# Forgetting attention and a tanh-shrink MLP in one kernel: seven MLP steps in four slots, and transposed q and k landing in tiles of their own

## The chip, the core and the metric

One core of a Trainium2 chip runs the whole program. The engines are TensorE (PE: matmuls; PEld: its weight loads), VectorE (DVE), ScalarE (ACT), GpSimd (POOL) and SyncE (SP), which only issues DMAs here. The metric is the device time of one execution in microseconds.

## What is computed

The reference, cut down (B = 8 batches, H = 8 heads, S = 576 positions, D = 64, so 4608 tokens of width 512; w_in is 512 x 2048, w_out 2048 x 512):

```python
scores = np.matmul(q, k.transpose(0, 1, 3, 2)) / np.sqrt(D)
cum = np.cumsum(np.log(np.clip(f, 0.0001, 1.0)), axis=-1)
decay = cum[:, :, :, None] - cum[:, :, None, :]
attn = softmax(np.where(causal, -1e9, scores + decay))
x = (attn @ v).transpose(0, 2, 1, 3).reshape(B * S, H * D)
h = x @ w_in
out = (h - np.tanh(h)) @ w_out
```

## The kernel before

**Slots.** Attention runs over 32 pairs of heads, four pairs for each batch, in the order of `pairs`. The loop at the end (L368) has 33 slots, p = 0 to 32. In slot p stand the scores of pair p (seven tiles, `scores`), the values of pair p-1 (`values`) and the turning of that pair's result into XR (`turn`, L291), with features on the partitions. XR (L67) is a ring of four batches.

**Units and steps.** The MLP is cut into nine units of 512 tokens, and each unit into 32 steps: 16 `mlp1` steps (L306: four matmuls into hps, tanh on ScalarE as th, the sum on VectorE as gt) and then 16 `mlp2` steps (L322: four matmuls into ops; after each fourth step one copy by ScalarE and one DMA of out). The list `mlp` (L365) holds them in order. From slot 5 on, each slot takes the next eight (`take`, L373) and strews them between its attention items; what is left after slot 32 runs alone, the tail. With eight to a slot, unit u starts with the first step of slot 5 + 4u. It reads XR rows of batch u, whose last pair is turned in slot 4u + 4.

**Order.** The order on TensorE, VectorE, GpSimd and SyncE is the order of the program (`manual_schedule`), and each of them works its queue off in order. An instruction that waits holds up everything behind it on its engine.

**q and k.** A batch's q and k stand with head dimension on the partitions in QT and KT, two buffers each (b % 2): rows 0 to 63 the data, rows 64 to 66 the decay and constants that go with a 67-row matmul (`lhsT=KT[...][0:D + 3]`, L258). Batches 0 to 2 are transposed on TensorE and copied out by VectorE (`trans`, L218 to L236), in slots 0 to 10. Batches from FAR = 3 on come by DMA. With p0 = 4(b-1): GpSimd loads the blocks of q in slot p0-1 and of k in slot p0 (`load_block`); SyncE issues five transposing DMAs for q in slot p0 and five for k in slot p0+1 (`turn_block`, L87). These land two heads at a time, on 128 partitions of the even heads' places of QT and KT; in slot p0+2 VectorE moves the lower 64 rows to the odd heads' places (`odd_heads`, L91, eight copies of 64x576). Since the transposes overwrite rows 64 to 127 of the even heads, slot p0+3 puts the constant rows back (`even_rows`, L154, two DMAs) and loads the decay rows (`load_aug`, L148, three DMAs). The table LOADS (L186 to L214) says after which tile of which slot each of these is emitted.

Of the kernel before, what the change touches and what calls it, by code (L numbers as in the profile page):

```python
# [9 lines left out]
FP16 = mybir.dt.float16  # L10
# [4 lines left out]
PITCH = 640  # L15
# [6 lines left out]
def kernel(  # L22
# [10 lines left out]
    nc = tc.nc  # L33
    P = 128

    B, H, S, D = q.shape
# [4 lines left out]
    NPAIR = H // 2  # L41
# [10 lines left out]
    qkp = ctx.enter_context(tc.tile_pool(name="qkp", bufs=1))  # L52
# [18 lines left out]
    qn, kn = ([t[0:S // NT6, :].rearrange("p (h n d) -> p h n d", h=H, n=NT6) for t in raw] for raw in (qraw, kraw))  # L71
    qb, kb = ([t[:, 0:NJ * DM].rearrange("p (n e) -> p n e", n=NJ) for t in raw] for raw in (qraw, kraw))
    vn = [qkp.tile([P, NJ, H, VW], FP16, tag=f"vn{i}", name=f"vn{i}") for i in range(2)]
    QT = [qkp.tile([P, H, S], FP16, tag=f"QT{i}", name=f"QT{i}") for i in range(2)]
    KT = [qkp.tile([P, H, PITCH], FP16, tag=f"KT{i}", name=f"KT{i}") for i in range(2)]

    def load_qk(dst, src, b, h0, h1):
        nc.gpsimd.dma_start(
            out=dst[b % 2][:, h0:h1, :, :].rearrange("p h n d -> p h (n d)"),
            in_=src[b, h0:h1, :, :].rearrange("h (p n) d -> p h (n d)", n=NT6))  # L80

    def load_block(dst, src, b, n):
        pn = min(P, S - n * P)
        nc.gpsimd.dma_start(out=dst[b % 2][0:pn, n, :].rearrange("p (h d) -> p h d", h=H),  # L84
                            in_=src[b, :, n * P:n * P + pn, :].rearrange("h p d -> p h d"))

    def turn_block(dst, src, b, n):  # L87
        pn = min(P, S - n * P)
        nc.sync.dma_start_transpose(out=dst[b % 2][:, 0:H:2, n * P:n * P + pn], in_=src[b % 2][0:pn, n, :])

    def odd_heads(dst, b, c):  # L91
        nc.vector.tensor_copy(out=dst[b % 2][0:D, 2 * c + 1, 0:S], in_=dst[b % 2][D:P, 2 * c, 0:S])

    def load_v_rest(b):
        nc.gpsimd.dma_start(out=vn[b % 2][0:S % P, NJ - 1, :, 0:D],
                            in_=v[b, :, S - S % P:S, :].rearrange("h p d -> p h d"))

    def load_v_head(b, h):
        nc.gpsimd.dma_start(out=vn[b % 2][:, 0:NJ - 1, h, 0:D],
                            in_=v[b, h, 0:S - S % P, :].rearrange("(n p) d -> p n d", p=P))  # L100

    def load_v_block(b, n, h0, h1):
        nc.gpsimd.dma_start(out=vn[b % 2][:, n, h0:h1, 0:D],  # L103
                            in_=v[b, h0:h1, n * P:(n + 1) * P, :].rearrange("h p d -> p h d"))
# [11 lines left out]
    ones16 = cst.tile([NH, S], FP16)  # L116
    nc.vector.memset(ones16, 1.0)
    minus16 = cst.tile([2 * H, S], FP16)
# [11 lines left out]
    for i in range(2):  # L130
        nc.vector.memset(KT[i][:, :, S:PITCH], 0.0)
    cum = cst.tile([NH, S], FP32)
# [15 lines left out]
    def load_aug(b):  # L148
        i, hs = b % 2, slice(b * H, (b + 1) * H)
        nc.sync.dma_start(out=KT[i][D:D + 1, :, 0:S], in_=chi[hs, :])  # L150
        (nc.gpsimd if b == 0 else nc.sync).dma_start(out=QT[i][D + 2:D + 3, :, :], in_=cq[hs, :])
        nc.sync.dma_start(out=KT[i][D + 1:D + 2, :, 0:S], in_=clo[hs, :])

    def even_rows(i):  # L154
        nc.sync.dma_start(out=QT[i][D:D + 2, 0:H:2, :], in_=minus16[0:H, :])
        nc.sync.dma_start(out=KT[i][D + 2:D + 3, 0:H:2, 0:S], in_=ones16[0:H // 2, :])

    def const_rows(i):
        nc.sync.dma_start(out=QT[i][D:D + 2, :, :], in_=minus16)
        nc.sync.dma_start(out=KT[i][D + 2:D + 3, :, 0:S], in_=ones16[0:H, :])  # L160

# [16 lines left out]
    def load_win(f0, f1):  # L178
        nc.gpsimd.dma_start(out=win[:, :, f0:f1],
                            in_=moe_w_in[:, f0:f1].rearrange("(c p) f -> p c f", p=P))  # L180

    def load_wout(t0, t1):
        nc.gpsimd.dma_start(out=wout[:, t0:t1, :],
                            in_=moe_w_out[t0 * P:t1 * P, :].rearrange("(t p) e -> p t e", p=P))

    LOADS = {(0, 1): [lambda: load_qk(qn, q, 1, 0, 2), lambda: load_qk(kn, k, 1, 0, 2)],  # L186
             (0, 4): [lambda: load_qk(qn, q, 1, 2, H)],
             (1, 0): [lambda: load_qk(kn, k, 1, 2, H)],
             (1, 2): [lambda: load_win(0, DFF // 2)],
             (1, 5): [lambda: load_v_rest(1), lambda: load_v_head(1, 0)],  # L190
             (2, 1): [lambda: load_v_head(1, 1), lambda: load_win(DFF // 2, DFF)],
             (4, 0): [lambda: load_wout(0, NFT // 2)],
             (4, 2): [lambda: load_wout(NFT // 2, NFT)]}
# [4 lines left out]
    for b in range(2, B):  # L198
        p0 = (b - 1) * NPAIR
        for n in range(NJ - 1):  # L200
            LOADS.setdefault((p0 + 1, n), []).append(lambda b=b, n=n: load_v_block(b, n, 0, H))
        LOADS.setdefault((p0 + 1, 4), []).append(lambda b=b: load_v_rest(b))
        if b < FAR:
            LOADS.setdefault((p0, 0), []).append(lambda b=b: load_aug(b))
            continue
        for n in range(NJ):
            LOADS.setdefault((p0 - 1, n), []).append(lambda b=b, n=n: load_block(qb, q, b, n))
            LOADS.setdefault((p0, n), []).append(lambda b=b, n=n: load_block(kb, k, b, n))
            LOADS.setdefault((p0, 4), []).append(lambda b=b, n=n: turn_block(QT, qb, b, n))
            LOADS.setdefault((p0 + 1, 4), []).append(lambda b=b, n=n: turn_block(KT, kb, b, n))  # L210
        for c in range(NPAIR):
            LOADS.setdefault((p0 + 2, c), []).append(lambda b=b, c=c: odd_heads(QT, b, c))
            LOADS.setdefault((p0 + 2, 3 + c), []).append(lambda b=b, c=c: odd_heads(KT, b, c))
        LOADS.setdefault((p0 + 3, 0), []).append(lambda b=b: (even_rows(b % 2), load_aug(b)))  # L214

    E, XN, GT, M2 = {}, {}, {}, {}

# [30 lines left out]
    def scores(b, c, ti):  # L248
        ps = ps_sc.tile([P, 512], FP32, tag="sc", name="ps")
        if ti == LAST:  # L250
            e = EL[(b * NPAIR + c) % 3]
        else:
            e = aex.tile([P, 512], FP16, tag="e", name="e")
        lo = min(x[4] for x in TILES[ti])
        hi = max(x[4] + x[3] for x in TILES[ti])
        for a, j, i0, n, col in TILES[ti]:
            h = 2 * c + a
            nc.tensor.matmul(out=ps[:, col:col + n], lhsT=KT[b % 2][0:D + 3, h, j * P:(j + 1) * P],  # L258
                             rhs=QT[b % 2][0:D + 3, h, i0:i0 + n])
            for ib in range(j, NJ):  # L260
                w0 = min(ib * P, S - P)
                if i0 <= ib * P < i0 + n:
                    E[(b, c, a, j, ib)] = e[:, col + w0 - i0:col + w0 - i0 + P]
        nc.scalar.activation(out=e[:, lo:hi], in_=ps[:, lo:hi], func=AF.Exp, scale=qscale)  # L264
        col, cp, step, wd = MASKS[ti]
        view = e[:, col:col + (cp - 1) * step + wd]
        if cp == 1:
            pat = [[1, wd]]
        else:
            view = bass.AP(view.tensor, view.offset, [list(view.ap[0]), [step, cp], [1, wd]])  # L270
            pat = [[0, cp], [1, wd]]
        nc.gpsimd.affine_select(out=view, in_=view, compare_op=ALU.is_ge, fill=0.0,  # L272
                                base=0, pattern=pat, channel_multiplier=-1)
# [93 lines left out]
    with tc.manual_schedule(engines={PE, mybir.EngineType.Pool, mybir.EngineType.SP, mybir.EngineType.DVE}):  # L367
        for p in range(len(pairs) + 1):  # L368
            b, c = divmod(p, NPAIR)
            if p == 0:  # L370
                load_aug(1)
            items = att_items(p)
            take = 8 if p > NPAIR else 0  # L373
            mine = mlp[at:at + take]
            at += take
            first = 3 if p == NPAIR + 1 else 0
            given, n = 0, 0
            whole = sum(counts for _, counts in items)
            for emit, counts in items:
                emit()  # L380
                n += counts
                while n > first and given < len(mine) and given * (whole - first) < (n - first) * len(mine):
                    fn, *args = mine[given]
                    fn(*args)
                    given += 1
        for fn, *args in mlp[at:]:
            fn(*args)
# [28 lines left out]
```

## Time and profile before

| what | value |
|---|---|
| median of three runs | 377.35 us (376.13 to 380.36) |
| the profiled execution's own time | 376.38 us |
| its span, first to last instruction | 374.5 us |
| time outside the span | 1.88 us |
| mean granted TensorE clock | 0.981 |
| TensorE busy | 345.0 us, 92% of the span |
| VectorE, ScalarE, GpSimd busy | 190.8, 219.7, 162.5 us |

The span is what the trace covers; the execution's own time is 1.88 us more. A row of a list of groups gives source line, engine, operation and tiles (out<-in, with partitions x elements), its count, the total and the mean of one, and then the idle time of that engine just before it with the instruction that ended it. Matmul records overlap: a 128x512 matmul is listed with 378 ns, but in an unbroken row one starts each 216 ns (64 of them took 13.81 us), so an MLP step of four takes 0.86 us.

### The profile page before, as it was taken

What the parts mean: (1) busy time and instruction counts of PE and PEld (TensorE: products, weight loads), DVE (VectorE), ACT (ScalarE), POOL (GpSimd) and SP (SyncE); (2) the same over time, 40 slices, a digit from 0 to 9 for tenths busy, and PEclk for the clock granted to TensorE, in tenths of its full rate; (3) what the DMA queues carried; (4) which work ended last, traced back from release to release, by engine and by line L of the source; (5) the groups of instructions that cost most, each with busy time, mean ns of one, the idle gap of its engine ahead of it and who ended that gap; (6) DMA issues with size and microseconds to landing.
All of it is one profiled execution on the core that took longest, in us unless ns stands there. A gap on an engine that the chain in (4) does not pass through costs nothing.

```text
span 374.5 us, 7401 instructions
## 1 busy us (share of the span) xinstructions
PE 345.0 (92%) x2724; PEld 188.6 (50%) x2724; DVE 190.8 (51%) x352; ACT 219.7 (59%) x411; POOL 162.5 (43%) x340
## 2 busy tenths in 40 slices
PE   1778999989899999979998999799999999999995
PEld 0556555545445455545556865355555554444442
DVE  7589688448941584137613771069117612721720
ACT  6565576558745785568655865478558832623721
POOL 7978723655166636644475547552222210000000
PEclk9997699999999999999999999899999999999999
DMA  8999999999879996999599959994220022002002
GB/s 104 157 175 192 204 178 91 128 130 147 76 71 140 140 147 69 137 133 149 44 140 150 129 72 140 141 132 71 74 75 18 16 74 72 3 28 84 2 28 84
DMA packets 140801, 38.79 MB, mean 104 GB/s; under 512 B 128114, under 2 KB 135070, under 8 KB 140766
## 3 DMA queue, kind: packets, MB, share of 16 engines
q0 software_dynamic: 92416, 18.37, 65.5%
q1 hardware_dynamic: 48350, 19.96, 28.1%
q8 instruction: 21, 0.34, 0.4%
q14 instruction: 14, 0.11, 0.1%
HBM read 36.85 MB, written 9.44 MB: 124 GB/s over the span
## 4 chain that ended last, share of the span: by engine, by line
PE 73%; DVE 10%; DMA 9%; ACT 4%; issue 2%; POOL 2%; SPq 0%; POOLq 0%; ACTq 0%; DVEq 0%
PE ops L328 28%; PE hps L314 27%; PE ps L258 9%; PE av L282 8%; DMA XR<-xn 7%; DVE gt L320 3%; DVE KT L236 2%; ACT e L264 1%; ACT th L317 1%; DVE QT L236 1%; DVE xn L288 1%; ACT ost L332 1%; PE t L227 1%; DMA lf<-in_f_dram 1%; DMA KT<-clo 1%
## 5 line engine op out<-in xcount | busy, mean ns | idle before, releaser
L264 ACT ACTIVATE e<-ps 128x512 f16<-128x512 f32 x192 | 110.9, 596 | 70.0 <-PE ps L258 68.7
L314 PE MATMUL hps<-XR,win 128*128 128x512 f16 (+1 forms) x640 | 142.1, 360 | 7.6 <-DMA XR<-xn 7.2
L320 DVE TENSOR_TENSOR gt<-hps,th 128x512 f16<-128x512 f32 x144 | 98.1, 690 | 91.0 <-ACT th L317 89.8
L328 PE MATMUL ops<-wout,gt 128*128 128x512 f16 x576 | 138.4, 378 | 0.0
L272 POOL TENSOR_SCALAR_AFFINE_SELECT e<-e 128x128 f16<-128x128 f16 (+1 forms) x192 | 64.6, 339 | 128.8 <-ACT e L264 126.5
L317 ACT ACTIVATE th<-hps 128x512 f32<-128x512 f32 x144 | 86.4, 600 | 42.1 <-PE hps L314 34.0
L258 PE MATMUL ps<-QT,KT 67*128 67x64 f16 (+4 forms) x384 | 79.4, 289 | 10.9 <-DMA KT<-clo 4.4
L314 PEld LDWEIGHTS <-win 128*128 128x128 f16 x640 | 58.5, 98 | 51.4 <-issue 2.2
L328 PEld LDWEIGHTS <-gt 128*128 128x128 f16 x576 | 52.2, 97 | 54.1 <-issue 0.2
L258 PEld LDWEIGHTS <-KT 67*128 67x128 f16 x384 | 37.6, 101 | 56.0 <-issue 18.6
L332 ACT ACTIVATE ost<-ops 128x512 f32<-128x512 f32 x36 | 21.5, 597 | 36.3 <-PE ops L328 29.2
L282 PEld LDWEIGHTS <-e 128*128 128x128 f16 x896 | 34.9, 101 | 8.6 <-POOL e L272 2.4
L282 PE MATMUL av<-vn,e 128*128 128x65 f16 x896 | 36.3, 199 | 1.4 <-POOL e L272 1.4
L286 DVE TENSOR_SCALAR rs<-av 128x10 f32<-128x10 f32 x32 | 5.3, 165 | 58.6 <-PE av L282 58.5
L103 POOL DMA_DIRECT2D vn<-in_v_dram x32 | 28.0, 876 | 2.3 <-issue 1.7
L288 DVE TENSOR_TENSOR xn<-av,rs 128x640 f16<-128x640 f32 x32 | 26.4, 825 | 1.1
L84 POOL DMA_DIRECT2D kn<-in_k_dram x25 | 21.2, 847 | 2.0 <-issue 1.8
L84 POOL DMA_DIRECT2D qn<-in_q_dram x25 | 21.2, 848 | 1.9 <-issue 1.5
L236 DVE COPY QT<-t 64x576 f16<-64x576 f16 x22 | 17.7, 804 | 7.5 <-PE t L227 7.3
L236 DVE COPY KT<-t 64x576 f16<-64x576 f16 x24 | 19.1, 796 | 4.1 <-PE t L227 3.9
L282 PE MATMUL av<-vn,el 128*128 128x65 f16 x64 | 12.7, 199 | 0.0
L272 POOL TENSOR_SCALAR_AFFINE_SELECT el<-el 128x128 f16<-128x128 f16 x32 | 9.9, 308 | 5.2 <-ACT el L264 5.0
(44 smaller groups left out, 95.5 us busy)
## 6 DMA issues: line engine op xcount, KB each, us to landing
out_dram<-ost SPq DMA_DIRECT2D x36, 256.0 KB
vn<-in_v_dram POOLq DMA_DIRECT2D x24, 128.0 KB, 5.4
qn<-in_q_dram POOLq DMA_DIRECT2D x20, 128.0 KB, 4.5
kn<-in_k_dram POOLq DMA_DIRECT2D x20, 128.0 KB, 4.5
win<-in_moe_w_in_dram POOLq DMA_DIRECT2D x2, 1024.0 KB, 11.3
wout<-in_moe_w_out_dram POOLq DMA_DIRECT2D x2, 1024.0 KB, 13.2
XR<-xn SPq DMA_TRANSPOSE x56
vn<-in_v_dram POOLq DMA_DIRECT2D x12, 64.0 KB, 4.9
```

What stands on the lines that cost most here:

```text
L84: nc.gpsimd.dma_start(out=dst[b % 2][0:pn, n, :].rearrange("p (h d) -> p h d", h=H), in_=src[b, :, n * P:n * P + pn, :].rearrange("h p d - ...
L103: nc.gpsimd.dma_start(out=vn[b % 2][:, n, h0:h1, 0:D], in_=v[b, h0:h1, n * P:(n + 1) * P, :].rearrange("h p d -> p h d"))
L236: nc.vector.tensor_copy(out=to, in_=of)
L258: nc.tensor.matmul(out=ps[:, col:col + n], lhsT=KT[b % 2][0:D + 3, h, j * P:(j + 1) * P], rhs=QT[b % 2][0:D + 3, h, i0:i0 + n])
L264: nc.scalar.activation(out=e[:, lo:hi], in_=ps[:, lo:hi], func=AF.Exp, scale=qscale)
L272: nc.gpsimd.affine_select(out=view, in_=view, compare_op=ALU.is_ge, fill=0.0, base=0, pattern=pat, channel_multiplier=-1)
L282: nc.tensor.matmul(out=av[:, a, ib, :], lhsT=E.pop((b, c, a, j, ib)), rhs=vn[b % 2][:, j, 2 * c + a, 0:D + 1], start=(j == 0), stop=(j == ib))
L288: nc.vector.tensor_tensor(out=xn.rearrange("p i (a d) -> p a i d", a=2), in0=av[:, :, :, 0:D], in1=rs.to_broadcast([P, 2, NJ, D]), op=ALU. ...
L314: nc.tensor.matmul(out=hps[:, o:o + n], lhsT=win[:, ci, ft * P:(ft + 1) * P], rhs=XR[:, ci, t:t + n], start=(ci == 0), stop=(ci == NCH - 1))
L317: nc.scalar.activation(out=th, in_=hps, func=AF.Tanh, scale=-1.0)
L320: nc.vector.tensor_tensor(out=gt, in0=hps, in1=th, op=ALU.add)
L328: nc.tensor.matmul(out=ops, lhsT=GT[(u, ft)][:, m * P:(m + 1) * P], rhs=wout[:, ft, :], start=(ft == 0), stop=(ft == NFT - 1))
```

## The change

Three things. Slots 6 to 9 take seven MLP steps instead of eight, so that units 1 to 6 start in the middle of a slot, four steps later, and four more steps stand in the tail. The transposing DMAs land in two tiles of their own, TQ and TK (128 partitions, four pairs), each with one buffer; in slot p0+3 eight copies of VectorE (`place`) move them to rows 0 to 63 of QT and KT, even and odd heads, two heads at a time. So nothing overwrites rows 64 to 66 any more: `even_rows` is gone, and `load_aug` moves from slot p0+3 to slot p0. QT and KT have 67 partitions instead of 128.

```diff
@@ QT and KT are made @@
-    QT = [qkp.tile([P, H, S], FP16, tag=f"QT{i}", name=f"QT{i}") for i in range(2)]
-    KT = [qkp.tile([P, H, PITCH], FP16, tag=f"KT{i}", name=f"KT{i}") for i in range(2)]
+    QT = [qkp.tile([D + 3, H, S], FP16, tag=f"QT{i}", name=f"QT{i}") for i in range(2)]
+    KT = [qkp.tile([D + 3, H, PITCH], FP16, tag=f"KT{i}", name=f"KT{i}") for i in range(2)]
+    TQ = qkp.tile([P, NPAIR, S], FP16, tag="TQ", name="TQ")
+    TK = qkp.tile([P, NPAIR, S], FP16, tag="TK", name="TK")
@@ turn_block, odd_heads @@
-        nc.sync.dma_start_transpose(out=dst[b % 2][:, 0:H:2, n * P:n * P + pn], in_=src[b % 2][0:pn, n, :])
-
-    def odd_heads(dst, b, c):
-        nc.vector.tensor_copy(out=dst[b % 2][0:D, 2 * c + 1, 0:S], in_=dst[b % 2][D:P, 2 * c, 0:S])
+        nc.sync.dma_start_transpose(out=dst[:, :, n * P:n * P + pn], in_=src[b % 2][0:pn, n, :])
+
+    def place(dst, src, b, a, c):
+        nc.vector.tensor_copy(out=dst[b % 2][0:D, 2 * c + a:2 * c + 3 + a:2, 0:S], in_=src[a * D:(a + 1) * D, c:c + 2, :])
@@ even_rows is left out; LOADS @@
+        LOADS.setdefault((p0, 0), []).append(lambda b=b: load_aug(b))
         if b < FAR:
-            LOADS.setdefault((p0, 0), []).append(lambda b=b: load_aug(b))
             continue
...
-            LOADS.setdefault((p0, 4), []).append(lambda b=b, n=n: turn_block(QT, qb, b, n))
-            LOADS.setdefault((p0 + 1, 4), []).append(lambda b=b, n=n: turn_block(KT, kb, b, n))
-        for c in range(NPAIR):
-            LOADS.setdefault((p0 + 2, c), []).append(lambda b=b, c=c: odd_heads(QT, b, c))
-            LOADS.setdefault((p0 + 2, 3 + c), []).append(lambda b=b, c=c: odd_heads(KT, b, c))
-        LOADS.setdefault((p0 + 3, 0), []).append(lambda b=b: (even_rows(b % 2), load_aug(b)))
+            LOADS.setdefault((p0, 4), []).append(lambda b=b, n=n: turn_block(TQ, qb, b, n))
+            LOADS.setdefault((p0 + 1, 4), []).append(lambda b=b, n=n: turn_block(TK, kb, b, n))
+        for n, (dst, src) in enumerate(((QT, TQ), (KT, TK))):
+            for a in range(2):
+                for c in (0, 2):
+                    LOADS.setdefault((p0 + 3, 2 * n + a), []).append(lambda b=b, dst=dst, src=src, a=a, c=c: place(dst, src, b, a, c))
@@ the loop over slots @@
-            take = 8 if p > NPAIR else 0
+            take = 0 if p <= NPAIR else 7 if NPAIR + 1 < p <= 2 * NPAIR + 1 else 8
```

Two places show how this moves the instructions. First VectorE, for batch 4 (p0 = 12), before: slot 14 and the start of slot 15. The row with seven gt reaches back into slot 13; rs and xn are the values of one pair; QT_97 and KT_99 are the buffers of even batches.

```order
L320 TENSOR_TENSOR gt<-hps,th 128x512 x7
L92 COPY QT_97<-QT_97 64x576
...
L288 TENSOR_TENSOR xn<-av,rs 128x2x5x64
L320 TENSOR_TENSOR gt<-hps,th 128x512 x2
L92 COPY QT_97<-QT_97 64x576
L320 TENSOR_TENSOR gt<-hps,th 128x512
L92 COPY KT_99<-KT_99 64x576
L92 COPY QT_97<-QT_97 64x576
L320 TENSOR_TENSOR gt<-hps,th 128x512 x2
L92 COPY KT_99<-KT_99 64x576
L320 TENSOR_TENSOR gt<-hps,th 128x512
L92 COPY KT_99<-KT_99 64x576 x2
```

The same batch in the changed program, slot 15 (the seven gt begin in slot 14):

```order
L318 TENSOR_TENSOR gt<-hps,th 128x512 x7
L94 COPY QT_97<-TQ 64x2x576 x2
L318 TENSOR_TENSOR gt<-hps,th 128x512
L94 COPY QT_97<-TQ 64x2x576 x2
L284 TENSOR_SCALAR rs<-av 128x10
L285 RECIPROCAL rs<-rs 128x10
L286 TENSOR_TENSOR xn<-av,rs 128x2x5x64
L318 TENSOR_TENSOR gt<-hps,th 128x512 x2
L94 COPY KT_99<-TK 64x2x576 x4
```

Eight copies that stood scattered among the gt of slot 14 are now eight copies of twice the size, one slot later, in a slot with about four gt: two pairs around one gt, and four in a row behind the unit's last gt.

Second SyncE, in the slots 15 and 16 before (out_dram is a block of the result and ost its copy, XR<-xn the turning of a pair, QT_98<-qn_92 the first transposes for batch 5):

```order
L155 DMA QT_97<-minus_114 2x4x576
L156 DMA KT_99<-ones_112 1x4x576
L150 DMA KT_99<-chi 1x8x576
L151 DMA QT_97<-cq 1x8x576
L152 DMA KT_99<-clo 1x8x576
L334 DMA out_dram<-ost 128x512
L302 DMA_TRANSPOSE XR<-xn 128x4x128
L304 DMA_TRANSPOSE XR<-xn 128x64
L334 DMA out_dram<-ost 128x512 x2
L302 DMA_TRANSPOSE XR<-xn 128x4x128
L304 DMA_TRANSPOSE XR<-xn 128x64
L89 DMA_TRANSPOSE QT_98<-qn_92 128x4x128 x4
```

And in the changed program, from the turning in slot 15 through slot 16:

```order
L300 DMA_TRANSPOSE XR<-xn 128x4x128
L302 DMA_TRANSPOSE XR<-xn 128x64
L332 DMA out_dram<-ost 128x512
L152 DMA KT_100<-chi 1x8x576
L153 DMA QT_98<-cq 1x8x576
L154 DMA KT_100<-clo 1x8x576
L332 DMA out_dram<-ost 128x512
L300 DMA_TRANSPOSE XR<-xn 128x4x128
L302 DMA_TRANSPOSE XR<-xn 128x64
L91 DMA_TRANSPOSE TQ<-qn_92 128x4x128 x4
L91 DMA_TRANSPOSE TQ<-qn_92 128x4x64
L332 DMA out_dram<-ost 128x512 x2
```

The five small DMAs ahead of slot 15's turning are gone, and three of them (for the next batch) stand in slot 16. The turning of slot 16, which ends batch 3 and which unit 3 waits for, stands as before behind one block of the result that is copied in the middle of the slot; the unit's steps that read it come half a slot later.

More of the change, by code (lines that the diff above doesn't have):

```diff
@@ L152, in load_aug @@
         nc.sync.dma_start(out=KT[i][D + 1:D + 2, :, 0:S], in_=clo[hs, :])
-    def even_rows(i):
-        nc.sync.dma_start(out=QT[i][D:D + 2, 0:H:2, :], in_=minus16[0:H, :])
-        nc.sync.dma_start(out=KT[i][D + 2:D + 3, 0:H:2, 0:S], in_=ones16[0:H // 2, :])
     def const_rows(i):
@@ L257, in scores @@
             h = 2 * c + a
-            nc.tensor.matmul(out=ps[:, col:col + n], lhsT=KT[b % 2][0:D + 3, h, j * P:(j + 1) * P],
-                             rhs=QT[b % 2][0:D + 3, h, i0:i0 + n])
+            nc.tensor.matmul(out=ps[:, col:col + n], lhsT=KT[b % 2][:, h, j * P:(j + 1) * P],
+                             rhs=QT[b % 2][:, h, i0:i0 + n])
             for ib in range(j, NJ):
```

## The prediction

> **What bounds the kernel now.** I read the page's busy times first, then TensorE's waits, then where those waits lie, then the busy times by slot.
>
> ```profile
> PE 345.0 (92%) x2724; PEld 188.6 (50%) x2724; DVE 190.8 (51%) x352; ACT 219.7 (59%) x411; POOL 162.5 (43%) x340
> ```
>
> TensorE is the bound: it works 345.0 of 374.5 us. Only its 29.5 us of idle time, and time at a lowered clock, can be won. A step moved from one place to another, both limited by TensorE, wins nothing. The list of waits, for TensorE:
>
> ```profile
> PE hps L314 <- DMA XR<-xn: 7.2, 5, 2.2
> PE t L227 <- DMA qn<-in_q_dram: 5.0, 1, 5.0
> PE ps L258 <- DMA KT<-clo: 4.4, 1, 4.4
> PE ps L258 <- DVE KT L236: 4.0, 6, 1.6
> ```
>
> The 5.0 and the 4.4 are the first loads and stay. The 7.2 in five pieces and the 4.0 are what an order can change. The timeline of TensorE, cut to the instructions that waited, shows where they lie:
>
> ```profile
> 82.28 0.38 PE L314 MATMUL hps<-XR,win 128*128 128x512 f16 x1 [1.02 <-DMA XR<-xn]
> 91.66 0.39 PE L258 MATMUL ps<-QT,KT 67*128 67x512 f16 x1 [0.36 <-DVE KT L236]
> 99.66 1.02 PE L314 MATMUL hps<-XR,win 128*128 128x512 f16 x4 [0.28 <-DVE gt L320]
> 103.60 0.39 PE L258 MATMUL ps<-QT,KT 67*128 67x512 f16 x1 [1.62 <-DVE KT L236]
> 123.78 0.38 PE L314 MATMUL hps<-XR,win 128*128 128x512 f16 x1 [0.72 <-DMA XR<-xn]
> 163.04 0.38 PE L314 MATMUL hps<-XR,win 128*128 128x512 f16 x1 [2.19 <-DMA XR<-xn]
> 201.71 0.27 PE L314 MATMUL hps<-XR,win 128*128 128x256 f16 x1 [1.12 <-DMA XR<-xn]
> 240.90 0.47 PE L314 MATMUL hps<-XR,win 128*128 128x512 f16 x1 [2.10 <-DMA XR<-xn]
> ```
>
> The five waits for XR are the first steps of units 1 to 5, some 39 us (four slots) apart: three matmuls on the older pairs run, the fourth waits for the pair just turned. Around 90 to 104 us (slots 9 and 10) there are three others, all for VectorE, 2.26 us together. Busy times by stretch: slots 9, 10, 13, 14 and 16, each about from one pair's values to the next's:
>
> ```profile
> 84.20:95.00 10.80, 10.44 (x92) 5.56 (x90) 9.82 (x17) 8.59 (x17) 5.59 (x11) 1.00 1.70 146
> 95.00:105.94 10.94, 9.04 (x83) 4.80 (x82) 10.53 (x21) 7.14 (x14) 3.19 (x9) 1.00 0.49 47
> 125.25:134.48 9.23, 9.23 (x80) 4.89 (x77) 6.42 (x12) 7.63 (x16) 5.59 (x11) 1.00 1.68 146
> 134.48:143.73 9.25, 9.25 (x80) 4.88 (x77) 8.43 (x19) 7.45 (x15) 2.71 (x8) 1.00 0.58 85
> 152.96:164.50 11.54, 9.35 (x80) 4.87 (x77) 1.63 (x4) 5.18 (x10) 7.07 (x13) 1.00 1.34 135
> ```
>
> The columns are length, then busy time of PE, PEld, DVE, ACT, POOL, clock, DMA. An undisturbed slot is all TensorE, 9.23 of 9.23. Slots 9 and 10 are VectorE's (9.82 of 10.80 and 10.53 of 10.94): eight gt, the copies of a transposed pair and, in slot 10, the odd heads fall together. The slot ahead of a new unit is 11.54, its surplus the 2.19 of the wait.
>
> After the wait of 2.10 us the clock fell. Three neighbouring stretches there, and the one after the wait of 2.19:
>
> ```profile
> 237.40:240.81 3.41, 1.40 (x8) 0.60 (x7) 0.00 (x0) 1.71 (x4) 2.18 (x5) 1.00 1.87 151
> 240.81:244.20 3.39, 3.30 (x24) 1.81 (x24) 0.73 (x2) 1.68 (x3) 1.17 (x2) 0.53 1.28 149
> 244.20:247.60 3.40, 3.40 (x34) 1.94 (x32) 2.64 (x6) 1.80 (x4) 0.58 (x2) 0.96 1.01 147
> 162.80:166.20 3.40, 3.16 (x42) 2.00 (x42) 1.68 (x4) 1.68 (x3) 1.23 (x3) 1.00 1.75 134
> ```
>
> A granted clock of 0.53 over 3.39 us costs 0.47 x 3.39 = 1.6 us. One wait brought it, one just as long didn't.
>
> **The half slot: minus 7.2 and minus 1.6.** A unit's first mlp1 step comes four steps and one pair's values later: four steps of 0.86 us, 0.9 us of values and three scores of 0.2, about 5.0 us. XR keeps its place behind one block of the result that is copied in the middle of the slot. In slot 16, VectorE's and SyncE's rows:
>
> ```profile
> 154.37 0.82 DVE L288 TENSOR_TENSOR xn<-av,rs 128x640 f16<-128x640 f32 x1
> ```
> ```profile
> 156.94 1.22 SPq L302 DMA_TRANSPOSE XR<-xn  x1
> 158.21 1.40 SPq L304 DMA_TRANSPOSE XR<-xn  x1
> ```
>
> xn is ready at 155.2, the turning is issued from 156.94 to 159.6, and TensorE goes on at 163.04. The longest wait is 2.19, so the half slot leaves 5.0 - 2.2 = 2.8 us to spare. SyncE has new work ahead of it in that slot, the three decay rows:
>
> ```profile
> L150 SPq DMA_DIRECT2D KT<-chi x8: 634/634/662, 7.1 to 262.8; - x8
> ```
>
> 3 x 0.63 = 1.9 us from the slot's start, over before the block of the result that it waits for anyway (156.5), so it costs nothing here; with that cover gone, 1.9, still under 2.8. So all five waits go, 7.2 us, and with them the slow clock, 1.6. The four steps that slots 6 to 9 lose, 4 x 0.86 = 3.5 us, come back in the tail, which is all TensorE: zero. Only slot 6 is doubtful, where VectorE is nearly full; bounds 0 and +0.4, I take 0.
>
> The Trainium skill, in "TensorE: Matmul & The Clock Gate", Part 1, ties the slow clock to at least one idle window of about 3.4 us. The row above shows it after an idle piece of 2.10 us, so the trace is stricter than the page. If the page were right here, the dip would have another cause and could stay; that is the third rival.
>
> **Slots 9 and 10: minus 1.6.** Unit 1's mlp1 now takes half of slot 9, slot 10 and half of slot 11, and the odd heads of batch 3 leave slot 10 for slot 11, where no pair is transposed. Prices from the page's groups:
>
> ```profile
> L320 DVE TENSOR_TENSOR gt<-hps,th 128x512 f16<-128x512 f32 x144 | 98.1, 690 | 91.0 <-ACT th L317 89.8
> L236 DVE COPY KT<-t 64x576 f16<-64x576 f16 x24 | 19.1, 796 | 4.1 <-PE t L227 3.9
> L92 DVE COPY KT<-KT 64x576 f16<-64x576 f16 x20 | 6.5, 343 | 1.2 <-issue 0.5 <-DMA KT<-kn 0.3
> L288 DVE TENSOR_TENSOR xn<-av,rs 128x640 f16<-128x640 f32 x32 | 26.4, 825 | 1.1
> ```
>
> Slot 9 falls from eight gt to four, 2.8 us less; slot 10 loses 8 x 0.31 = 2.5 but keeps 8 x 0.69 + 4 x 0.80 + 1.2 for the values (0.825 and two short ones) = 9.9, still above TensorE's 9.04 there, and may hand some of it on to slot 11. Of the 2.26 us I count 1.6; bounds 0.5 and 2.3.
>
> **The copies: plus 1.0.** Forty copies of 64x576 become forty of 64x1152. No row has this shape. The nearest:
>
> ```profile
> L92 DVE COPY QT<-QT x20: 301/306/395, 94.3 to 258.7; 64x576 f16<-64x576 f16 x20
> L168 DVE COPY vn<-clo 64x1 f16<-64x1 f16 x4 | 0.3, 138 | 0.0
> ```
>
> Between 138 ns for one column and 301 for 576 lie 0.283 ns a column, which makes 138 + 1152 x 0.283 = 0.46 us. Slot 15 then has 8 x 0.46 = 3.7, about four gt (2.8) and the values (1.2), 7.7 of 9.23: it fits, as 8.43 fitted in slot 14. Bounds: 0.46, and 1.6 (twice the 0.80 of L236, which steps through its output). What is queued behind the copies: one gt behind each pair of QT copies, so that this gt and ScalarE's th two steps on are late by up to 0.9 us where 0.3 was usual; and behind the four KT copies only the next slot's values. The first scores of the new batch come after that and need only the first copies. The cover for a late gt is the three buffers of hps; if it isn't enough, TensorE waits up to the 0.6 us by which the copies grew, and per unit I put 0.2, five times 1.0 us; bounds 0 and 4.0. The even rows, ten DMAs of SyncE, go for nothing: no wait of TensorE's hangs on them.
>
> **The sum.** 374.5 - 7.2 - 1.6 - 1.6 + 1.0 = 365.1 us of span; with the 1.9 us around it 367.0. The profiled execution was 376.38, 1.0 under the median of 377.35; I take no correction, since that spread may itself be waits for XR and clock.
>
> **Rivals.**
>
> The copies meet GpSimd. They move from a slot in which GpSimd issues no loads (2.71 us busy, slot 14) to one in which it issues the next batch's q. The only copies of this trace beside such an issue are the last two in slot 10, VectorE's row and then GpSimd's:
>
> ```profile
> 105.36 1.01 DVE L92 COPY KT<-KT 64x576 f16<-64x576 f16 x2
> ```
> ```profile
> 105.00 0.89 POOL L84 DMA_DIRECT2D qn<-in_q_dram  x1
> ```
>
> 1.01 for two instead of 0.6, one of them 0.63. At 0.63 per 576 columns a copy takes 1.26 and slot 15's VectorE 10.1 + 2.8 + 1.2 = 14.1, 4.9 above 9.23. TensorE would wait that out before the new batch's scores, five times, 24 us: 366.0 + 24 = 390. It decides from (9.23 - 4.0) / 8 = 0.65 us a copy. For it: that row. Against it: one copy in 40, and five issues of 0.89 cover only half of the slot. The Trainium skill's "GPSIMD Engine Reference", section 1, says that GpSimd shares its SBUF interfaces with VectorE and contends with its two-port modes; the row agrees, and the page gives no price.
>
> The wait moves. With XR in time, TensorE meets VectorE or ScalarE in slots 11, 15, 19, 23 and 27, at the upper bound of 4.0 instead of 1.0, and slots 9 and 10 give only 0.5: 367.0 + 3.0 + 1.1 = 371.1. For it: the copies come two before a gt. Against it: in slot 14 eight gt and eight copies cost 0.02 us.
>
> The dip stays. Some lowered clock is met elsewhere: 367.0 + 1.6 = 368.6. For it: a wait of 2.19 left the clock alone. Against it: no other dip after 46 us but the one behind a wait.
>
> The waits stay. Something new holds XR up by more than 2.8 us: 374.5 - 1.6 + 1.0 + 1.9 = 375.8. Against it: its place on SyncE's queue is the old one.
>
> **How the numbers follow.** Forecast 0.60 (365 to 368); the dip stays 0.13; the wait moves 0.15; the waits stay 0.07; the copies meet GpSimd 0.05. All gains at their upper bounds and no cost give 374.5 - 7.2 - 1.6 - 2.3 + 1.9 = 365.3; with run-to-run spread the low end is 364.3. The high end takes in the moved wait: 371.6. Measurements of this kernel can tell about 1% (3.8 us): faster, below 373.6, is 0.60 + 0.13 + 0.15 less a little = 0.87; the same 0.08; slower 0.05.
>
> **What would show it.** Right: no row of TensorE waiting for XR among the longest, slots 12, 16, 20 and 24 at 9.2 to 9.5 us, a clock near 0.985 or above, place copies at 0.45 to 0.6 us, slots 9 and 10 shorter by 1 to 2 us together. Wrong: place copies above 0.65, TensorE waiting for VectorE in slots 11, 15 and on by over 0.5 us each, or XR waits still above 2 us in all.

## The result and the profile after

The changed kernel took 366.29 us (median of four runs, 365.61 to 367.73) beside 378.49 for the kernel before: a ratio of 0.969, with a 95% interval of 0.962 to 0.976, 3.1% faster. A second series of six runs gave 365.96 and a ratio of 0.971 (0.967 to 0.975). Forecast were 367.0 and a range of 364.3 to 371.6. The ratios leave out executions that ran in a slower state of the chip, the medians do not.

The profiled execution has a span of 366.0 us (367.73 in all). Its page, busy times:

```profile
PE 347.7 (95%) x2724; PEld 191.5 (52%) x2724; DVE 196.1 (54%) x352; ACT 218.1 (60%) x411; POOL 162.4 (44%) x340
```

Its list of TensorE's waits:

```profile
PE t L225 <- DMA qn<-in_q_dram: 5.8, 1, 5.8
PE ps L256 <- DMA KT<-clo: 3.9, 1, 3.9
PE ps L256 <- DVE KT L234: 1.6, 4, 0.6
```

No wait for XR is left. What is left is the start, and short waits for transposed blocks. TensorE's idle time fell from 29.5 to 366.0 - 347.7 = 18.3 us, by 11.2; its busy time rose by 2.7, for the same 2724 matmuls. Busy times by stretch: slots 9, 10, 15 and 16, from one pair's values to the next's (columns as in the prediction):

```profile
82.95:93.13 10.18, 9.92 (x93) 5.33 (x90) 7.49 (x13) 7.68 (x15) 5.47 (x11) 1.00 1.78 157
93.13:102.53 9.40, 8.76 (x83) 4.68 (x79) 8.20 (x14) 7.41 (x15) 3.11 (x8) 1.00 0.57 70
139.49:148.72 9.23, 9.23 (x80) 4.88 (x77) 6.95 (x15) 5.88 (x12) 6.71 (x13) 1.00 1.15 95
148.72:157.99 9.27, 9.27 (x80) 4.87 (x77) 1.21 (x3) 4.73 (x9) 6.43 (x13) 1.00 1.39 134
```

Slot 16, which was 11.54 us long, is 9.27 and all TensorE. Slot 15, which has the new copies, is 9.23 and all TensorE too, with 6.95 us of VectorE. The copies themselves, and SyncE's turning in slot 16 with the first matmuls that read it:

```profile
L94 DVE COPY QT<-TQ x20: 444/456/860, 102.7 to 252.7; 64x1152 f16<-64x1152 f16 x20
L94 DVE COPY KT<-TK x20: 441/456/684, 107.8 to 256.7; 64x1152 f16<-64x1152 f16 x20
```
```profile
152.67 1.27 SPq L300 DMA_TRANSPOSE XR<-xn  x1
153.99 1.22 SPq L302 DMA_TRANSPOSE XR<-xn  x1
```
```profile
160.75 1.46 PE L312 MATMUL hps<-XR,win 128*128 128x512 f16 x6
```

The turning is fully issued at 155.2. Unit 3 starts at 160.75 with three matmuls on older pairs; the fourth, at about 161.4 (3 x 0.216 us on), is the first that reads this pair, 6.2 us after the issue and without a wait. Before, 3.4 us passed from there (159.61) to the same matmul (163.04), which stood waiting. That leaves 2.8 us of room. (Unit 1 starts three steps later and not four: slot 9, in which it starts, is itself one of the four slots that lose a step.)

### The profile page after: what moved, and what is told of

It is laid out like the page before. It is cut to its first block, busy times and chain, and to the rows that moved or that the text cites. A ratio compares the mean times of both kernels' runs of the same rounds, so it can differ in the third digit from the quotient of the medians.

```text
span 366.0 us, 7384 instructions
## 1 busy us (share of the span) xinstructions
PE 347.7 (95%) x2724; PEld 191.5 (52%) x2724; DVE 196.1 (54%) x352; ACT 218.1 (60%) x411; POOL 162.4 (44%) x340
## 4 chain that ended last, share of the span: by engine, by line
PE 87%; DVE 6%; ACT 3%; DMA 2%; issue 1%; POOL 1%; POOLq 0%; ACTq 0%
PE ops L326 34%; PE hps L312 31%; PE ps L256 12%; PE av L280 9%; DVE KT L234 2%; DVE gt L318 2%; ACT e L262 2%; PE t L225 1%; ACT th L315 1%; DMA KT<-clo 1%; DMA lf<-in_f_dram 1%; DVE xn L286 0%; DVE QT L234 0%; POOL e L270 0%; DVE cum L135 0%
## 5 line engine op out<-in xcount | busy, mean ns | idle before, releaser
L256 PE MATMUL ps<-QT,KT 67*128 67x64 f16 (+4 forms) x384 | 81.0, 297 | 7.4 <-DMA KT<-clo 3.9
L256 PEld LDWEIGHTS <-KT 67*128 67x128 f16 x384 | 38.6, 103 | 47.6 <-issue 11.4
L280 PE MATMUL av<-vn,e 128*128 128x65 f16 x896 | 37.1, 201 | 0.8 <-POOL e L270 0.8
L225 PE MATMUL t<-id,qn 96*128 96x96 f16 x72 | 6.6, 243 | 5.8 <-DMA qn<-in_q_dram 5.8
## 6 DMA issues: line engine op xcount, KB each, us to landing
win<-in_moe_w_in_dram POOLq DMA_DIRECT2D x2, 1024.0 KB, 11.2
wout<-in_moe_w_out_dram POOLq DMA_DIRECT2D x2, 1024.0 KB, 11.2
```

The costliest lines, as they stand in the source:

```text
L256: nc.tensor.matmul(out=ps[:, col:col + n], lhsT=KT[b % 2][:, h, j * P:(j + 1) * P], rhs=QT[b % 2][:, h, i0:i0 + n])
L280: nc.tensor.matmul(out=av[:, a, ib, :], lhsT=E.pop((b, c, a, j, ib)), rhs=vn[b % 2][:, j, 2 * c + a, 0:D + 1], start=(j == 0), stop=(j == ib))
```

## The experiments

Each kernel ran on one chip beside the kernel before, whose medians there were 376.6 to 376.7 us.

**1. The half slot alone.** The kernel before with

```diff
-            take = 8 if p > NPAIR else 0
+            take = 0 if p <= NPAIR else 7 if NPAIR + 1 < p <= 2 * NPAIR + 1 else 8
```

> The kernel before with the half slot alone (seven MLP steps in slots 6 to 9); q and k land as before, with odd_heads, even_rows and the late load_aug. My theory, that the half slot carries the gain and the new landing next to nothing: no wait of TensorE for XR, 366 to 368.5 us; the odd heads stay in slot 10 among eight gt, so 1 to 2 us of waits for the KT copies stay in slots 9 and 10. Rival, that the half slot needs the new landing (VectorE and SyncE fall behind without it): XR waits or waits for VectorE of over 3 us stay, 371 us or more.

Measured: 380.05 us, ratio 1.010 (1.003 to 1.018). Not faster at all. TensorE's longest wait in its list, and VectorE's group of odd heads of k:

```profile
PE hps L314 <- DVE gt L320: 7.9, 5, 2.9
```
```profile
L92 DVE COPY KT<-KT 64x576 f16<-64x576 f16 x20 | 6.4, 338 | 10.9 <-DMA KT<-kn 6.9 <-issue 3.6
```

The five waits for XR (7.2 us) are gone, and five waits for gt (7.9) stand in their place; one of them (0.27, in slot 10) was there before. VectorE's idle time before the odd heads of k was 1.2 us before the change and is 10.9 here. One place, in slots 16 to 18: SyncE's transposes of q and k, then VectorE, then TensorE:

```profile
157.36 6.98 SPq L89 DMA_TRANSPOSE QT<-qn  x5
168.88 6.46 SPq L89 DMA_TRANSPOSE KT<-kn  x5
```
```profile
173.89 0.69 DVE L320 TENSOR_TENSOR gt<-hps,th 128x512 f16<-128x512 f32 x1
178.18 0.30 DVE L92 COPY KT<-KT 64x576 f16<-64x576 f16 x1 [3.60 <-issue]
178.74 0.69 DVE L320 TENSOR_TENSOR gt<-hps,th 128x512 f16<-128x512 f32 x1
```
```profile
179.49 1.02 PE L314 MATMUL hps<-XR,win 128*128 128x512 f16 x4 [2.88 <-DVE gt L320]
```

The copy runs 9.3 us after the first of the five DMAs was issued; VectorE was there at 174.6 and stood still for 3.6 us, a gt queued behind. (This row names no releaser; before the first odd heads of k of the batches beside it the waits are 2.26, 1.92 and 2.76 us, all for the DMA.) In the kernel before, SyncE and VectorE at the same place:

```profile
159.71 7.10 SPq L89 DMA_TRANSPOSE QT<-qn  x5
170.11 6.45 SPq L89 DMA_TRANSPOSE KT<-kn  x5
```
```profile
179.53 0.31 DVE L92 COPY KT<-KT 64x576 f16<-64x576 f16 x1 [0.54 <-issue]
```

Again 9.4 us from issue to copy, but VectorE came only 0.54 us too early. In both kernels SyncE works without a pause from the first transpose of q to the last of k: q's five, the result, the turning, k's five. In the kernel before TensorE's wait of 2.19 us for XR lies inside that stretch (it ends at 163.04), so it held TensorE and VectorE back while SyncE went on. Without it VectorE comes 2.2 us earlier; SyncE also has two blocks of the result ahead of k here instead of one (1.02 us instead of 0.53) and a slower turning. TensorE's waits at the other batches show the same:

```profile
139.15 1.02 PE L314 MATMUL hps<-XR,win 128*128 128x512 f16 x4 [1.54 <-DVE gt L320]
219.81 1.03 PE L314 MATMUL hps<-XR,win 128*128 128x256 f16 x8 [1.18 <-DVE gt L320]
259.32 1.60 PE L314 MATMUL hps<-XR,win 128*128 128x512 f16 x4 [2.03 <-DVE gt L320]
```

The four new waits, 1.54, 2.88, 1.18 and 2.03, in slots 14, 18, 22 and 26, come two slots after the waits for XR that went, 0.72, 2.19, 1.12 and 2.10, in slots 12, 16, 20 and 24. So the landing of k was late by a little before the change too, and by these traces the wait for XR covered the rest. My theory that the half slot carries the gain by itself falls. The waits don't add up to the 3.9 us, though: those for XR and gt together rose by 0.3. A second fall of the clock in the middle costs about 1.7 (the last section); the rest is open.

**2. The landing alone.** The changed kernel with `take = 8 if p > NPAIR else 0`.

> The changed kernel with eight steps in every slot: the new landing alone. My theory: five waits for XR of about 7 us in all stay, the waits in slots 9 and 10 fall from 2.3 to about 1 us, the copies cost nothing (slot 15 then has no gt): 376 to 378.5 us, within 1% of before. Rival, that the landing brings half of the gain or more by itself: below 373 us.

Measured: 373.64 us, ratio 0.995 (0.990 to 0.999), about 2 us. Its list of TensorE's waits:

```profile
PE hps L312 <- DMA XR<-xn: 8.8, 5, 2.2
PE ps L256 <- DVE KT L234: 3.0, 6, 0.9
```

The waits for XR stay, as expected. (The profiled execution, 376.59 us, is 3 us above the median.) The median is 2.4 us under the band that I gave: slots 9 and 10 lost their wait of 1.62 and have 0.36 each; the 0.9 here is at the start. Half slot alone +3.9 us at the ratio, landing alone -2.1, together -11.8: the two parts need each other.

**3. Two steps later instead of four.** The changed kernel with

```diff
-            take = 0 if p <= NPAIR else 7 if NPAIR + 1 < p <= 2 * NPAIR + 1 else 8
+            take = 0 if p <= NPAIR else 7 if NPAIR + 1 < p <= NPAIR + 3 else 8
```

> The changed kernel with seven steps in slots 6 and 7 alone, so that units 1 to 6 start two steps later than before instead of four, about 3.0 us (two steps, one pair's values, scores). My theory, that only the arrival of XR counts and was at most 2.2 us late: no wait for XR, or one or two below 0.5 us; 366 to 368 us. Rival, that XR needs more than the waits showed (its DMAs land later once nothing holds TensorE back): waits of over 2 us in all, 369 us or more.

Measured: 364.57 us, ratio 0.968 (0.963 to 0.974), and no wait for XR. Two steps are enough; the median is 1.4 us under the expected band.

**4. Every copy twice.** `place` is called twice in a row for each (a, c).

> The changed kernel with every place copy issued twice, the second writing the same values again: 80 copies of 64x1152, twice the work of VectorE in slots 11, 15, 19, 23 and 27. By the threshold of my prediction (0.65 us a copy; here two take about 1.0) VectorE's slot has 8 x 1.0 + 4.0 = 12 us of work in 9.23, and TensorE waits up to 2.8 us in each, 14 in all: 372 to 380 us. Rival, that the work runs over into the next slot, where VectorE has only 1.2 us to do, and that the new batch's first scores need only the first copies: under 3 us in all, 366 to 369 us.

Measured: 376.71 us, ratio 1.000 (0.996 to 1.004): 10 to 12 us slower than the changed kernel, inside the first theory's band. TensorE's waits are 6.7 us in all, where that theory had up to 14:

```profile
PE ops L327 <- DVE gt L319: 5.5, 13, 0.9
PE ps L257 <- DVE KT L94: 1.2, 5, 0.2
```

Most is a wait for gt, not for the new batch's QT and KT. VectorE in slot 15:

```profile
140.74 2.29 DVE L94 COPY QT<-TQ 64x1152 f16<-64x1152 f16 x4
142.95 0.68 DVE L319 TENSOR_TENSOR gt<-hps,th 128x512 f16<-128x512 f32 x1
143.65 2.57 DVE L94 COPY QT<-TQ 64x1152 f16<-64x1152 f16 x4
```

One gt stands behind 2.3 us of q's copies; the values of a pair and two more gt stand behind 2.6. VectorE has no pause in this slot from 140.13 to 152.56, and the slot lasts 11.4 us instead of 9.23. So this run alone doesn't tell what costs: the order of VectorE's queue, or that its work no longer fits into the slot.

**5. The copies a slot earlier.** The changed kernel with

```diff
-                    LOADS.setdefault((p0 + 3, 2 * n + a), []).append(lambda b=b, dst=dst, src=src, a=a, c=c: place(dst, src, b, a, c))
+                    LOADS.setdefault((p0 + 2, n * (3 + a) + a), []).append(lambda b=b, dst=dst, src=src, a=a, c=c: place(dst, src, b, a, c))
```

> The changed kernel with its place copies one slot earlier, in slot p0+2, where the odd heads stood (q after the first two score tiles, k after the fourth and sixth); own tiles, no even_rows, early load_aug and the half slot all stay. Theory after the first four runs: what the new landing gives is one slot more between the transposing DMAs and VectorE's first copy that needs them; then the first KT copy waits for its landing by 2 to 4 us with gt queued behind it, and TensorE waits for gt about 8 us in all: 375 to 381 us. Rival, that the gain lies in the five small DMAs of SyncE that are gone from slot p0+3 or in the constant rows: no such wait, 366 to 368 us.

Measured: 378.44 us, ratio 1.004 (0.999 to 1.009): the gain is gone, though `even_rows` is gone and `load_aug` early. (The profiled execution, 374.76 us, is the fastest of the ten.) TensorE's list and VectorE's group:

```profile
PE hps L312 <- DVE gt L318: 7.1, 10, 1.0
```
```profile
L94 DVE COPY KT<-TK 64x1152 f16<-64x1152 f16 x20 | 9.4, 510 | 6.4 <-DMA TK<-kn 6.3
```

So the slot of the copies carries the landing's share, and not SyncE's small DMAs. It does so in two ways that this run doesn't part: four of the ten waits (3.2 us) stand behind KT copies, which wait 6.3 us for their landing, four (2.9 us) behind QT copies that wait for nothing, one (1.0 us) lies in slot 10, where no copy waits, and the last is 0.1 us. That slot p0+2 has, by the prices, eight gt, the values and eight copies of 0.46: 5.5 + 1.2 + 3.7 = 10.4 us of VectorE in 9.23.

**6. One step later.** The changed kernel with seven steps in slot 7 alone.

> The changed kernel with seven steps in slot 7 alone, so that units 1 to 6 start one step later, about 1.1 us. The landing-only run waited 1.48, 1.58, 2.22, 2.06 and 1.46 us for XR. Theory, that XR's arrival does not depend on TensorE: each wait shrinks by about 1.1, to 0.4 to 1.1 us, 3 to 3.5 us in all and none over 2 us, so no fall of the clock in the middle: 368 to 371 us. Rival, that TensorE's later start also makes XR later: over 6 us of waits stay, 372 us or more.

Measured: 369.96 us, ratio 0.983 (0.977 to 0.988), and

```profile
PE hps L312 <- DMA XR<-xn: 5.7, 5, 1.5
```

The time is in the band, the sum of the waits isn't: 5.7 instead of 3 to 3.5. The waits shrank by 0.6 on the mean, from 8.8 / 5 to 5.7 / 5, and unevenly: 1.20, 1.52, 0.97, 0.66 and 1.33 us, so two by 1.25 and 1.40 and three by 0.06 to 0.28. XR's turning does depend on TensorE here: on SyncE's queue it stands behind a block of the result, and that block came a step later too. In slot 16 the turning is issued 2.69 us after xn is ready, in run 2 1.77 us after it. So the rival was right in part. No wait is over 2 us and the clock stayed up in the middle. With zero, one, two and four steps of delay the waits for XR are 8.8, 5.7, 0 and 0 us.

**7. The KT copies twice, the QT copies once.**

> The changed kernel with the four KT copies of each batch issued twice and the QT copies once: half of the added work of the run with all copies twice, and all of it behind the unit's last gt. Theory, that a copy costs only through the gt queued behind it: under 1.5 us of waits for VectorE in slots 11, 15 and so on, 365 to 368 us. Rival, that VectorE's total in the slot decides: half of the 10 us which all copies twice cost, 370 to 373 us.

Measured: 366.71 us, ratio 0.971 (0.966 to 0.975), the time of the changed kernel. TensorE waits for no gt behind a copy and for no copy. VectorE in slot 15 and the start of slot 16:

```profile
143.40 4.12 DVE L94 COPY KT<-TK 64x1152 f16<-64x1152 f16 x8
148.49 0.17 DVE L285 TENSOR_SCALAR rs<-av 128x10 f32<-128x10 f32 x1 [0.98 <-PE av L281]
```

The doubled copies end at 147.5, and VectorE then stands idle for 0.98 us until the next values. It is busy for 8.98 of this slot's 9.23 us, so the added work still fits, and it is free. So half of run 4's added work does not bring half of its cost. This doesn't settle what made run 4 slow: there q's copies are doubled too, with gt behind them, and VectorE's work no longer fits. The kernel with the copies of q alone doubled, which would tell the two apart, was not run.

**8. The first batch's scores twice.** In `scores`:

```diff
+            for _ in range(2 if b == 0 else 1):
-            nc.tensor.matmul(out=ps[:, col:col + n], lhsT=KT[b % 2][:, h, j * P:(j + 1) * P],
-                             rhs=QT[b % 2][:, h, i0:i0 + n])
+                nc.tensor.matmul(out=ps[:, col:col + n], lhsT=KT[b % 2][:, h, j * P:(j + 1) * P],
+                                 rhs=QT[b % 2][:, h, i0:i0 + n])
```

> The changed kernel with every score matmul of batch 0 (slots 0 to 3) issued twice into the same place, the second overwriting the first: more work for TensorE where it waits for others. It tests whether the half clock of 4 to 17 us around 25 to 45 us, which differs from run to run, comes from TensorE's idle pieces in slots 1 to 3. If so: no granted clock of 0.5 before 45 us, and 362 to 365 us. Rival, that it comes anyhow: the same fall of the clock, and 366 to 370 us, since the added matmuls then run at half clock too.

Measured: 366.87 us (366.57 to 370.29), ratio 0.975 (0.970 to 0.980): no gain. Its granted clock by slices, and that of the changed kernel:

```profile
PEclk9999999999999999999999999999999999999999
```
```profile
PEclk9995599999999999999999999999999999999999
```

In the one profile of this kernel the clock doesn't fall at the start, but the added matmuls seem to take the time that this saves: TensorE is busy for 346.5 us, 347.7 in the changed kernel's first profile. The mean clocks of its four executions are 0.994 to 0.999, those of the changed kernel's ten 0.976 to 0.993. It fits that idle pieces bring the fall; four executions don't settle it.

**9. The half slot with k turned earlier.** The first kernel, and the five transposes of k after the second score tile of slot p0+1:

```diff
-            LOADS.setdefault((p0 + 1, 4), []).append(lambda b=b, n=n: turn_block(KT, kb, b, n))
+            LOADS.setdefault((p0 + 1, 1), []).append(lambda b=b, n=n: turn_block(KT, kb, b, n))
```

> The half slot with the old landing, as in the first run, but the five transposing DMAs of k are issued after the second score tile of slot p0+1 instead of the fifth, ahead of one block of the result and of that slot's turning on SyncE's queue. Theory: in the first run VectorE's odd heads of k waited 10.5 us in all for these DMAs, with gt queued behind; issued 3 us earlier they have landed, the wait for gt falls below 2 us, and the half slot's gain appears without the new landing: 366 to 370 us. Rival, that the old place of the copies among eight gt is itself too full once TensorE doesn't stand still: over 5 us of waits for gt stay, 375 us or more.

Measured: 366.66 us, ratio 0.973 (0.969 to 0.977). SyncE in slot 17, VectorE's group and TensorE's list:

```profile
161.12 6.87 SPq L89 DMA_TRANSPOSE KT<-kn  x5
```
```profile
L92 DVE COPY KT<-KT 64x576 f16<-64x576 f16 x20 | 6.2, 330 | 0.5
```
```profile
PE ps L258 <- DVE KT L236: 3.5, 6, 1.5
PE hps L314 <- DVE gt L320: 0.3, 1, 0.3
```

From the first transpose of q (152.81 in this trace) to the first of k it is 8.3 us here, 11.5 in run 1. With k issued earlier the odd heads wait 0.5 us in all instead of 10.9, and the half slot gives nearly all of the gain with the old landing, the old place of the copies and the five small DMAs. This shows the cause of run 1: the landing of k. The wait of 1.5 in slot 10 stays, as no copy left that slot.

**10 to 12. The changed kernel again, two steps later again, and a rearranged end.** The last is the kernel of run 3 with

```diff
             given, n = 0, 0
+            while p == len(pairs) and given < 2:
+                fn, *args = mine[given]
+                fn(*args)
+                given += 1
```

> The changed kernel unchanged, beside the two that follow on the same chip: 365.5 to 367.5 us.

> Seven steps in slots 6 and 7 alone, again: within 1.5 us of the changed kernel (theory: no wait for XR in either, and nothing else depends on where in a slot a unit starts). Rival, that it is truly faster by 2 us, as the two single series suggested (364.6 against 366.3).

> The same with two MLP steps of slot 32 ahead of the last pair's values, which wait 0.6 to 0.8 us for GpSimd's last mask in every profile so far: that wait goes and nothing else moves; 0.6 to 0.8 us below the kernel with seven steps in slots 6 and 7. Rival, that the last turning now comes two steps later and the last unit but one waits for XR: same or slower.

Measured, six runs each on one chip: 365.96 (ratio 0.971, 0.967 to 0.975), 364.21 (0.968, 0.964 to 0.972) and 363.70 (0.966, 0.962 to 0.969). The kernel with two steps is the faster by 1.75 us here, more than the 1.5 that I had allowed, and was by 1.7 in the first runs of both. The intervals overlap, and why is open: about 1.4 us of it is in the profiles (spans of 361.7 and 360.3), without a wait that differs by as much. From the last xn to the end it is 69.1 and 67.4 us, the two steps fewer of the tail; ahead of that xn these two steps cost only 0.3. The last is the fastest of all; its profile has no wait for GpSimd in slot 32, but its 0.5 us over run 11 is within the spread of either.

## Why the prediction was right

**The sum held, its division didn't.** The span was to fall by 9.4 us and fell by 8.5: 11.2 us less of idle time (XR 7.2, transposed blocks 2.4, the rest small pieces), and 2.7 us more of busy time, which fits the lower clock at the start (below).

**The waits for XR, -7.2:** gone, as forecast, and the 2.8 us of room held. But the prediction put this on the half slot by itself, and run 1 shows the half slot alone at 1% slower than before. The step that failed is "the half slot: minus 7.2 and minus 1.6", which asked of XR alone what comes late next: alone it left 7.9 us of waits for gt and a time 3.9 us longer. The wait for XR covered VectorE's wait for k's landing. The prediction quotes the row, for another purpose: the odd heads of k had 1.2 us of idle time before them, part of it ended by the DMA. A copy that waits half a microsecond for its DMA is a second deadline, and it hardly shows until the first is taken away. Of my rivals "the wait moves" had the right kind (a wait for VectorE in place of XR) and the wrong place and cause; it came true in the kernel that I didn't predict.

**The copies, +1.0: 0, and a gain that I missed.** The price of one was right (0.46 forecast, 456 ns at the median, 0.51 on the mean, with one of 0.86 in slot 11; in slot 27, where GpSimd issues no loads, the KT copies took 441 to 456 ns). But I counted the move of the copies from slot p0+2 to p0+3 as a cost only. That slot of delay is what lets k land in time (run 5 without it: 378.44; run 9 with an earlier issue in its place: 366.66). It also takes them from among eight gt to among four. The rival that the copies meet GpSimd fell: 0.51 is under its threshold of 0.65 us a copy. The threshold itself, which came from VectorE's total in the slot, stands untested: run 7 stays under that total and costs nothing, run 4 goes over it and costs ten us, but its gt also stand behind the copies of q.

**Slots 9 and 10, -1.6:** the three waits of 2.26 became two of 0.26 and 0.64, so -1.36. Run 9, the half slot with the odd heads still in slot 10, keeps 2.05 of them; run 2, without the half slot, has only 0.72: it was the copies' leaving and not the half slot that won this.

**The clock, -1.6:** the fall at 241 us is gone with the wait before it. In this execution the gain was eaten up at the start, and the sign that I named, a clock near 0.985 or above, did not come: it was 0.977. The kernel before and the changed one, from 25 to 46 us:

```profile
25.00:37.00 12.00, 9.39 (x122) 6.65 (x122) 10.78 (x18) 7.62 (x17) 9.82 (x22) 0.83 1.41 192
37.00:46.00 9.00, 8.87 (x72) 5.41 (x71) 5.63 (x10) 5.05 (x10) 7.07 (x15) 0.66 1.38 202
```
```profile
25.00:37.00 12.00, 10.82 (x122) 8.15 (x121) 9.83 (x18) 7.18 (x14) 9.26 (x21) 0.64 1.40 191
37.00:46.00 9.00, 8.71 (x68) 5.45 (x67) 6.27 (x11) 4.62 (x9) 6.28 (x13) 0.53 1.39 195
```

The time lost to the lower clock is at most 0.17 x 12 + 0.34 x 9 = 5.1 us in the one and 0.36 x 12 + 0.47 x 9 = 8.6 in the other, over work that the change doesn't touch; at most, because TensorE also stands idle in these stretches. A second profile of the changed kernel, with a fall of 0.14 x 12 = 1.7 us there, had a span of 361.7, 4.3 us less, and 363.47 us in all. So the start seems to move a run by several us, and that the forecast met the median to within one is partly luck. The sum took 0.9 us too much off the profiled execution, and that one is the slowest of its four. Two errors of opposite sign stand in it: the cost of 1.0 that didn't come, and the 2.7 us of slower matmuls that did.

## What to carry to other kernels

When a wait is taken away, look at every transfer that lands while the engine stands there: the copy that finds its data just in time, with half a microsecond of idle time ended by a DMA, is the next wait. Two edits that look like one gain and one harmless move can be one gain only together, so test each alone before you put the gain on either. On an engine that works in order, price a copy by the room in its slot and by what is queued behind it: two more microseconds of copies a batch were free behind the last gt, where they still fitted; two more on top, in front of gt and past the slot's room, cost some ten us over five batches.

## What the runs showed of the hardware

The granted clock fell to about one half after short idle pieces of TensorE. In the middle of the program six waits of over 2 us are in the traces of before and of runs 1 and 2 (2.03, 2.06, 2.10, 2.19, 2.22, 2.88), and five of them were followed by some 3.4 us at half clock, all but that of 2.19; of those of 1.6 us and less none was. Run 1 around its wait of 2.88, and run 2 around its 2.06:

```profile
180.00:182.00 2.00, 1.85 (x9) 0.68 (x8) 1.88 (x6) 2.00 (x5) 1.16 (x3) 0.78 0.01 5
182.00:184.00 2.00, 2.00 (x32) 1.72 (x31) 1.15 (x2) 0.68 (x2) 1.68 (x3) 0.50 0.48 33
```
```profile
203.00:205.00 2.00, 2.00 (x12) 1.32 (x10) 0.69 (x1) 1.08 (x2) 0.59 (x2) 0.50 1.49 130
205.00:207.00 2.00, 2.00 (x36) 1.95 (x35) 0.99 (x3) 0.60 (x1) 0.58 (x1) 0.68 1.12 148
```

The Trainium skill, "TensorE: Matmul & The Clock Gate", Part 1, asks for an idle window of about 3.4 us; the length of the fall agrees with that window, the idle time needed was shorter. So a wait of 2 us cost up to 3.7 here, and one of 1.5 cost 1.5.
